# A conformer block on one core: full chunks' rows transposed by VectorE and DMAs in place of TensorE

## The chip, the core and the metric

The kernel runs on one NeuronCore of a Trainium2 chip. The time is device microseconds of one execution of the whole program. Three runs of the kernel before took 914.69, 914.84 and 915.0 us; the median is 914.84 us.

The engines are named as the profile names them: PE (TensorE, matrix multiplication; PEld is its loading of weights), ACT (ScalarE), DVE (VectorE), POOL (GpSimd), SP (SyncE, which here only issues DMAs). Results of PE go to PSUM, eight banks of 512 float32 per partition. Everything else lies in SBUF, 128 partitions.

## What is computed

A block of a speech encoder over x of 2 sequences x 4000 tokens x 144 features, 4 heads, all tensors in bf16:

```python
h = _layernorm(x); x = x + 0.5 * (_silu(h @ w_ff1a) @ w_ff1b)        # 144 -> 576 -> 144
h = _layernorm(x); qkv = h @ w_qkv                                   # 3 x 144, 4 heads of 36
p = _softmax(einsum('bhqd,bhkd->bhqk', q, k) * 36 ** -0.5)           # 4000 x 4000 per head
x = x + einsum('bhqk,bhkd->bhqd', p, v) @ w_o
h = _layernorm(x) @ w_pw1; h = h[..., :144] * _sigmoid(h[..., 144:])
x = x + _silu(depthwise_conv5(h, dw)) @ w_pw2                        # 5 taps along the tokens
h = _layernorm(x); x = x + 0.5 * (_silu(h @ w_ff2a) @ w_ff2b)
return _layernorm(x)
```

## The kernel before

**Tiling.** The 8000 tokens are 16 chunks of 500 (8 to a sequence); a chunk is four blocks of 125 tokens. X holds rows: 125 partitions, one token each, 144 features along. A layer norm (`ln`, line 704) takes sums with `bn_stats` on DVE, the inverse root as a power on POOL, and writes normalised rows XN. In the "calm" stages (the front, until keys and values of all eight chunks of the first sequence are there; and the tail, after the last score tile) DVE writes XN; between them POOL does, with 224 instructions in all.

**Transposing.** Every matmul that contracts over the features wants them on partitions. So `transp` (line 693) turns the rows: per block two PE transposes, 125 tokens x 72 features to 72 x 125, into one PSUM bank; then one copy of 72 x 1000 by DVE (ACT in calm stages where it is freer) to XT, or to XTQ for the projections. `ln_tr` and `ln_trq` (lines 749, 756) call it on normalised rows; `post1` (line 1089) calls it on AN, the attention's output rows. The features lie as 72 + 72, and each product is two matmuls of contraction 72 (`mm2`, line 783). The identity the transposes multiply with is IDENT; IDF is its float32 copy, made by one DVE cast in the setup and used in `epilogue` (line 1292), which turns the attention's sums back to rows, divides them and writes AN.

**Attention.** A score tile is 64 keys x 500 queries x 4 heads: four matmuls PS<-QT,KT into two banks, which run side by side on quarters of the array. `emit_exp` (line 1371) takes the exponential of both banks in one ACT instruction, 128 x 1000, into PT; four matmuls PS<-PT,VA then add weighted values in banks 6 and 7. Some tiles go to DVE instead (`dve_tile`, line 1385): five DVE instructions build the exponential as a sum of two parts from the bits of an int16, and since that gives two PT buffers, eight PS<-PT,VA matmuls follow in place of four. Of 992 full tiles ACT takes 825 and DVE 167.

**The order of the work** is made while the program is built. A planner (`Rec`, line 51; `Sched`, line 259) keeps a clock per engine, a cost per instruction, and how long after it a result can be read. Everything but the attention is written as generators ("threads") that ask for an engine and buffers; `pick_any` (line 1524) chooses at each step a score tile, an exp, a value product, or a thread's next piece. `due` (line 1611) says when a tile goes to DVE. What is chosen is appended to that engine's list. On the chip each engine works its own list in order, and an instruction waits for the semaphores of those it depends on. POLICY (line 373) holds the tables by which the planner chooses, one value for each 21 score tiles; FJ and TJ break ties in the front and the tail. Where the planner sees PE wait in the calm stages it fills in dummy matmuls PS<-IDENT (`warm`, line 611).

**Setup.** Lines 568 to 600: SP loads X of the first eight chunks, ACT's queue the first weights, POOL and DVE clear buffers, DVE makes IDF. POOL's list then goes on with the powers of the first layer norms.

**The SP queue** issues X's loads and the late weights until 22 us, then only the output's stores.

The transposing before, whose callers hand it rows and a place:

```python
for k in range(2):
    for i in range(n):
        op("pe", "transpose", ps[:, k, i, 0:rows], src[:, i, k * HD:(k + 1) * HD], IDENT[0:rows, 0:rows],
           r=[rk, "ID"], w=[("ps", bk)], cost=0.055, kind="f")
yield need("dve", hold=True)
copy(dst.rearrange("p k (i n) -> p k i n", i=n), ps[:, :, :, 0:rows], [("ps", bk)], wk, 2 * n * TB, 2.0, flex())
```

All engines' instructions are issued through one helper, so that the profile has them under one line (L170); groups are told apart by their tiles.

Of the kernel before, what the change touches and what calls it, by code (L numbers as in the profile page):

```python
# [12 lines left out]
D = 144  # L13
H = 4
DH = 36
# [27 lines left out]
def c_act(n):  # L43
    return n / 1200 + 0.051
# [6 lines left out]
class Rec:  # L51
# [6 lines left out]
    SWITCH = 0.095  # L58
# [12 lines left out]
    def op(self, eng, name, *a, r=(), w=(), q=None, cost=0.1, kind=None, lat=None, **k):  # L71
# [29 lines left out]
        if eng == "pe":  # L101
            if kind != self.kind:
                start += self.SWITCH
            self.kind = kind
# [4 lines left out]
        self.ops.append(o)  # L109
        return o  # L110
# [141 lines left out]
class Thread:  # L252
    def __init__(self, gen, ready, rank, no=0):
        self.no = no
        self.gen, self.ready, self.live, self.rank = gen, ready, True, rank
        self.req = None
# [67 lines left out]
def bass_standalone__conformer_family_zipformer__speech_kernel(  # L324
# [28 lines left out]
    def sb(name, shape, dt=BF16):  # L353
# [5 lines left out]
    NAN = 5  # L359
    TJ = (  # L360
        0.0, -0.6, 0, 0.0, -0.3, 0.0, 0.0, 0.0, 0.0, -0.6, 0.15, 0.15, -0.6, 0.0, 0.15, 0,
        0.0, 0.0, 0.0, 0.0, 0.0, 0.0, 0.3, 0.6, 0.6, -0.3, -0.3, 0.0, 0.0, 0.0, 0.0, 0.0,
        0.0, 0.0, 0.0, 0.15, 0.0, 0.0, 0.0, -0.15, 0.0, 0.0, 0.0, 0.0, 0, 0.6, 0.0, 0.0,
    )
    FJ = (
        0.0, 0.0, 0.0, 0.0, 0.0, 0.0, 0.0, 0.0, 0.0, 0.0, 0.0, 0.0, 0.0, 0.0, 0.0, 0.0,
        0.0, 0.0, 0.0, 0.0, 0.0, 0.0, 0.0, 0.0, 0.0, 0.0, 0.0, 0.0, 0, 0.0, 0.0, 0.0,
        -0.25, 0.0, 0.0, 0.0, 0.0, 0.0, 0.0, 0.0, 0.0, 0.0, 0, 0.0, 0.0, 0.0, 0.0, 0.0,
        0.0, 0.0, 0.0, 0.0, 0.0, 0.0, 0.0, 0.0, 0.0, 0.0, 0.0, 0.0, 0.0, 0.0, 0.0, 0.0,
    )  # L370
# [4 lines left out]
            0.56, 0.56, 0.56, 0.85, 0.85, 0.85, 0.56, 0.56, 0.56, 0.56, 0.56, 0.56, 1.0, 1.0, 0.56, 0.56,  # L375
            0.56, 0.56, 0.56, 0.56, 0.56, 0.56, 0.56, 0.56, 0.56, 0.6, 0.6, 0.5, 0.5, 0.5, 0.5, 0.56,
            0.56, 0.56, 0.56, 0.56, 0.56, 0.56, 0.56, 0.56, 0.5, 0.5, 0.56, 0.56, 0.56, 0.56, 0.56, 0.56,
            0.56,
        ),
        "DSLACK": (  # L380
            0.4, 0.4, 0.4, 2.5, 1.5, 1.5, 1.5, 1.0, 1.0, 1.5, 0.8, 0.4, 0.4, 0.4, 0.2, 0.2,
            0.4, 0.4, 0.4, 0.4, 1.5, 1.5, 1.5, 1.5, 4.0, 4.0, 4.0, 0.4, 0.4, 0.2, 0.4, 0.4,
            0.4, 0.4, 0.4, 0.4, 0.4, 0.4, 0.2, 0.2, 0.2, 0.4, 0.4, 0.4, 0.4, 1.5, 1.5, 1.5,
# [3 lines left out]
            2.0, 2.0, 4.0, 3.5, 4.5, 4.5, 4.5, 2.5, 2.5, 2.5, 2.5, 2.5, 2.5, 2.5, 2.5, 2.5,  # L387
            2.5, 2.5, 2.5, 2.5, 4.5, 2.5, 2.5, 2.5, 2.5, 2.5, 3.0, 3.25, 3.25, 3.0, 6.0, 3.25,
            3.25, 3.25, 3.25, 3.25, 4.0, 2.5, 2.5, 2.5, 3.25, 3.25, 3.25, 4.5, 4.5, 4.5, 3.25, 3.25,
# [3 lines left out]
            3, 3, 1, 1, 4, 4, 1, 1, 1, 3, 0, 0, 0, 0, 1, 1,  # L393
            1, 1, 1, 1, 1, 1, 1, 1, 1, 1, 1, 2, 1, 1, 1, 1,
            1, 1, 1, 1, 1, 1, 0, 0, 0, 0, 0, 1, 2, 0, 0, 1,
            1,
        ),
        "OBATCH": (
            1, 1, 2, 1, 1, 1, 1, 1, 1, 1, 1, 1, 1, 1, 1, 1,
            1, 1, 1, 1, 1, 1, 1, 1, 0, 2, 2, 2, 2, 2, 2, 1,  # L400
            1, 1, 1, 1, 1, 1, 2, 1, 1, 1, 1, 1, 1, 1, 3, 2,
            2,
        ),
        "LATE": (
            0.3, 0.3, 0.3, 0.3, 0.6, 0.6, 0.1, 0.2, 0.2, 0.2, 0.2, 0.2, 0.6, 0.6, 0.6, 0.1,
            0.1, 0.1, 0.1, 0.1, 0.1, 0.3, 0.3, 0.3, 0.3, 0.3, 0.2, 0.2, 0.2, 0.3, 0.3, 0.3,
            0.3, 0.3, 0.2, 0.2, 0.2, 0.2, 0.2, 0.2, 0.2, 0.2, 0.2, 0.2, 0.2, 0.2, 0.2, 0.2,
# [3 lines left out]
            1.8, 1.8, 1.6, 1.6, 1.6, 1.6, 1.6, 2.0, 2.5, 2.5, 2.5, 2.5, 2.5, 1.4, 2.5, 2.5,  # L411
            2.5, 1.8, 2.5, 2.5, 2.5, 1.6, 1.6, 1.6, 1.6, 1.6, 1.6, 1.4, 1.4, 1.4, 1.4, 3.5,
            3.5, 3.5, 3.5, 2.5, 2.5, 1.4, 1.4, 1.4, 1.6, 1.6, 3.0, 3.0, 1.4, 1.4, 1.4, 1.8,
# [3 lines left out]
            2, 2, 2, 2, 2, 2, 2, 2, 2, 3, 3, 3, 3, 3, 2, 2,  # L417
            5, 5, 4, 2, 2, 3, 2, 2, 2, 2, 2, 2, 2, 4, 2, 4,
            4, 5, 5, 2, 2, 2, 4, 5, 5, 5, 5, 5, 5, 5, 5, 4,
            3,  # L420
        ),
        "LIVE": (
            3, 3, 2, 2, 1, 1, 1, 1, 1, 2, 2, 2, 2, 3, 3, 3,
            3, 2, 2, 2, 2, 3, 3, 2, 2, 1, 1, 2, 2, 3, 3, 3,
            3, 3, 3, 3, 3, 3, 2, 3, 3, 4, 3, 3, 3, 3, 3, 3,
            3,
        ),
        "MAXQ": (
            2, 2, 3, 3, 1, 1, 3, 2, 1, 1, 1, 1, 1, 1, 3, 2,
            3, 3, 2, 2, 1, 2, 2, 2, 2, 1, 1, 2, 2, 2, 2, 2,  # L430
            2, 2, 2, 2, 2, 2, 3, 1, 1, 1, 3, 3, 3, 3, 3, 3,
            3,
        ),
        "EARLY": (
            2, 2, 2, 1, 3, 3, 2, 2, 2, 2, 2, 2, 2, 1, 1, 1,
            2, 2, 1, 1, 2, 2, 2, 2, 2, 2, 2, 2, 2, 2, 2, 2,
            2, 1, 1, 2, 2, 2, 3, 3, 3, 3, 3, 3, 2, 2, 2, 2,
# [3 lines left out]
            0.12, 0.12, 0.12, 0.12, 0.05, 0.05, 0.3, 0.12, 0.12, 0.05, 0.05, 0.05, 0.05, 0.05, 0.12, 0.12,  # L441
            0.12, 0.12, 0.12, 0.12, 0.12, 0.12, 0.12, 0.12, 0.12, 0.12, 0.12, 0.12, 0.2, 0.2, 0.2, 0.12,
            0.3, 0.2, 0.2, 0.2, 0.2, 0.2, 0.12, 0.12, 0.12, 0.12, 0.12, 0.12, 0.12, 0.12, 0.12, 0.12,
            0.12,
        ),
        "TWIN": (
            0.1, 0.1, 0.1, 0.1, 0.1, 0.1, 0.1, 0.1, 0.1, 0.1, 0.1, 0.1, 0.1, 0.1, 0.1, 0.1,
            0.1, 0.1, 0.1, 0.1, 0.1, 0.1, 0.1, 0.1, 0.0, 0.0, 0.0, 0.1, 0.1, 0.1, 0.1, 0.1,
            0.1, 0.1, 0.1, 0.1, 0.1, 0.1, 0.1, 0.1, 0.1, 0.1, 0.1, 0.1, 0.1, 0.1, 0.1, 0.1,
            0.1,  # L450
        ),
        "BGPICK": (
            0, 0, 0, 0, 0, 0, 0, 0, 0, 0, 0, 0, 0, 0, 0, 0,
            0, 0, 0, 0, 0, 0, 0, 0, 0, 0, 0, 0, 0, 0, 0, 0,
            1, 1, 1, 0, 0, 0, 1, 0, 0, 0, 0, 0, 0, 0, 0, 0,
# [3 lines left out]
            2, 2, 2, 1, 2, 2, 2, 2, 2, 0, 0, 0, 0, 0, 2, 2,  # L459
            2, 2, 2, 2, 2, 2, 2, 2, 2, 2, 2, 2, 2, 2, 0, 0,  # L460
            2, 2, 2, 2, 2, 3, 2, 2, 2, 2, 2, 2, 2, 2, 2, 2,
            2,
        ),
        "FDVE": (
            5, 5, 5, 5, 5, 5, 5, 5, 5, 5, 5, 5, 4, 4, 4, 5,
            5, 3, 3, 3, 3, 5, 5, 5, 5, 5, 5, 5, 5, 2, 2, 5,
            5, 5, 5, 5, 5, 5, 5, 5, 5, 5, 5, 5, 5, 1, 5, 5,
            5,
        ),
        "PRELAG": (  # L470
            0.7, 0.7, 0.7, 0.7, 0.7, 1.0, 0.7, 1.5, 1.5, 0.7, 0.7, 0.7, 0.7, 0.7, 0.7, 0.7,
            0.7, 0.7, 0.7, 0.7, 0.7, 0.7, 0.7, 0.7, 0.7, 0.7, 0.7, 1.0, 1.0, 1.0, 1.0, 0.7,
            0.7, 0.5, 0.5, 0.5, 0.5, 0.5, 0.7, 0.3, 0.3, 0.3, 0.7, 0.7, 0.5, 0.5, 0.5, 0.5,
            1.0,
        ),
        "LAGD": (
            1, 1, 1, 1, 1, 1, 1, 0, 0, 0, 0, 0, 1, 1, 0, 1,
            1, 1, 1, 1, 1, 1, 1, 1, 1, 1, 1, 1, 1, 0, 0, 0,
            1, 1, 1, 1, 1, 1, 1, 1, 1, 1, 1, 0, 0, 0, 0, 1,
# [19 lines left out]
    XN = sb("XN", [NXN, NB, D])  # L499
# [4 lines left out]
    XT = sb("XT", [NXT, 2, CW])  # L504
# [11 lines left out]
    AN = sb("AN", [NAN, NB, D])  # L516
# [24 lines left out]

    PS = nc.alloc_psum_tensor("PS", [128, 8 * 512], F32)
# [14 lines left out]

    def load_x(eng, c, r=()):
        load(eng, f"x{c}", X[0:TB, c * NB:(c + 1) * NB, :], x_tok[c], [("X", c, i) for i in range(NB)], r, 2.9)

    def load_ff(eng, qa, qb, WA, WE, WB, wa, wb, nm, la=None, lb=None):
        load(eng, qa, WA[0:HD, :, :], kh(wa)[:, :, 0:512], [(nm, "a", 0)], lat=la)
        load(eng, qa, WE[0:HD, :, 64:128], kh(wa)[:, :, 512:FF], [(nm, "a", 1)], lat=la)
        load(eng, qb, WB[:, 0:4, :], wb[0:512, :].rearrange("(t p) d -> p t d", p=128), [(nm, "b", 0)], lat=lb)
        load(eng, qb, WB[0:64, 4, :], wb[512:FF, :], [(nm, "b", 1)], lat=lb)
        load(eng, qb, WB[64:128, 5, :], wb[512:FF, :], [(nm, "b", 2)], lat=lb)

    load_x("sp", 0)
# [7 lines left out]
    op("pool", "memset", NHALF[:, :], -0.5, w=["NHALF"])  # L576
    op("pool", "memset", WP2Z[:, :, :], 0.0, w=[("WP2Z", i) for i in range(NB)], cost=0.3)
    op("pool", "memset", U2[:, :, :], 0.0, w=["U20"], cost=0.6)
    load("sp", "w2", WO[0:HD, :, :], kh(w_o), ["WO"])
    load("sp", "w2", WP1[0:HD, :, :], kh(w_pw1), ["WP1"])  # L580
# [9 lines left out]
    for WE, WB, nm, eng in ((WE1, WB1, "W1", "dve"), (WE2, WB2, "W2", "pool")):  # L590
        op(eng, "memset", WE[0:HD, :, 0:64], 0.0, w=[(nm, "a", 2)], cost=0.15)
        op(eng, "memset", WE[0:HD, :, 128:192], 0.0, w=[(nm, "a", 3)], cost=0.15)
# [61 lines left out]
    def setup_dw():  # L654
        for ab in range(2):
            op("dve", "tensor_copy", WPZ[0:HD, :, 48 + 64 * ab:64 + 64 * ab], WP1[0:HD, :, ab * D + ML:(ab + 1) * D],
               r=["WP1", "WPZ0"], w=["WPZ"], cost=0.15)
# [35 lines left out]
    def transp(src, rk, dst, wk, n, rows=TB):  # L693
        bk = yield need("pe", banks, dur=0.11 * n)
        ps = PSH[0:HD, bk, 0:256 * n].rearrange("p (k i n) -> p k i n", k=2, i=n)
        for k in range(2):
            for i in range(n):
                op("pe", "transpose", ps[:, k, i, 0:rows], src[:, i, k * HD:(k + 1) * HD], IDENT[0:rows, 0:rows],
# [1007 lines left out]
```

## Time and profile before

| | |
|---|---|
| median of 3 runs | 914.84 us (914.69 to 915.0) |
| the profiled execution | 914.9 us, its span 913.1 us |
| TensorE clock granted | 0.999 |
| ACT, exp of 128 x 1000 | 825 instructions, 768.8 us busy |
| PE, PS<-QT,KT and PS<-PT,VA | 3968 and 4636 instructions, 415.6 and 396.1 us busy |
| PE, transposes PS<-IDENT,XN and PS<-IDENT,AN | 512 and 128 instructions |
| DVE, copies XT<-PS and XTQ<-PS of 72 x 1000 | 51 and 8 instructions, mean 673 and 671 ns |
| DVE, the exps' three kinds of instruction | 222.4 + 134.7 + 113.0 us busy |
| DMA | 7322 packets, 7.36 MB |

How to read it: busy time of a group is the time in which at least one of its instructions is running, so instructions that overlap in a pipeline are not counted twice; the mean is that of a single record and holds its latency. The "idle before" column tells how long the engine had stood still ahead of the group and what ended that. A stretch's row gives, for every engine, the busy time in that stretch and the number of instructions. The chain of waits goes back from the last instruction, at each step to what released it.

### The profile page before, as it was taken

Reading aid. Unit: us, or ns where it says so; the run is one execution under the profiler, and the core shown is the slowest. Engines: PE = TensorE matmul, PEld = TensorE weight load, DVE = VectorE, ACT = ScalarE, POOL = GpSimd, SP = SyncE. Lnnn points to the kernel's source line nnn. Section 1 sums busy time; section 2 is a strip of 40 time slices with the busy share of each in tenths; the row PEclk is TensorE's granted clock in tenths of the full one; section 3 lists DMA queues with packets and bytes.
Section 4 is the critical chain, followed back from the end, with each engine's and each line's share of the span. In section 5 each row is a group of like instructions: output and inputs, shape, how many; then the busy total and the mean of one; then the engine's idle time right before and its main releaser. Section 6 shows DMA issues by size and latency. Waiting matters only on the chain.

```text
span 913.1 us, 27439 instructions
## 1 busy us (share of the span) xinstructions
PE 890.1 (97%) x11946; PEld 411.2 (45%) x11946; DVE 802.0 (88%) x1756; ACT 872.9 (96%) x1105; POOL 277.5 (30%) x519
## 2 busy tenths in 40 slices
PE   8999999999999999999999999999999999999996
PEld 7544434444444444444444444444434344444455
DVE  8988898898989999898988799897889699978987
ACT  5899999999999999999999999999999999999984
POOL 5121041145111612223415333240605050403143
PEclk9999999999999999999999999999999999999999
DMA  4000000000000000000000000000000000000000
GB/s 114 34 2 1 2 2 1 1 3 1 3 3 1 3 2 2 2 3 1 2 2 14 1 9 8 8 2 1 15 1 2 8 9 2 8 1 8 2 8 26
DMA packets 7322, 7.36 MB, mean 8 GB/s; under 512 B 2376, under 2 KB 7202, under 8 KB 7202
## 3 DMA queue, kind: packets, MB, share of 16 engines
q1 hardware_dynamic: 5786, 5.00, 1.8%
q8 instruction: 93, 1.52, 0.7%
q10 hardware_dynamic: 1416, 0.62, 0.3%
q14 instruction: 27, 0.22, 0.1%
HBM read 3.31 MB, written 2.30 MB: 6 GB/s over the span
## 4 chain that ended last, share of the span: by engine, by line
ACT 51%; PE 43%; DVE 4%; issue 1%; DMA 0%; POOL 0%; POOLq 0%; DVEq 0%
ACT PT L170 46%; PE PS L170 43%; ACT TH L170 5%; DVE HT L170 1%; DVE PT L170 1%; DVE ST L170 1%; DMA X<-in_x_dram 0%; DVE X L170 0%; DVE XN L170 0%; DVE QT L170 0%; POOL RS L170 0%; DVE XT L170 0%; DVE RS L170 0%; DVE SW L170 0%; DVE VA L170 0%
## 5 line engine op out<-in xcount | busy, mean ns | idle before, releaser
L170 ACT ACTIVATE PT<-PS 128x1000 bf16<-128x1000 f32 (+1 forms) x841 | 777.2, 1050 | 8.3 <-PE PS L170 5.9
L170 PE MATMUL PS<-QT,KT 64*64 64x500 bf16 x3968 | 415.6, 383 | 8.6 <-ACT PT L170 5.6
L170 PE MATMUL PS<-PT,VA 64*37 64x500 bf16 x4636 | 396.1, 373 | 1.9 <-DVE QT L170 1.4
L170 DVE TENSOR_SCALAR PT<-PS 128x500 int16<-128x500 f32 x334 | 222.4, 671 | 31.5 <-PE PS L170 29.5
L170 PEld LDWEIGHTS PS<-QT,KT 64*64 64x64 bf16 x3968 | 123.8, 104 | 195.7 <-ACT PT L170 112.5
L170 PEld LDWEIGHTS PS<-PT,VA 64*37 64x37 bf16 x4636 | 132.1, 95 | 111.3 <-issue 26.7
L170 POOL TENSOR_SCALAR RS<-ST 125x4 f32<-125x4 f32 x112 | 36.6, 327 | 471.0 <-DVE ST L170 465.8
L170 DVE TENSOR_SCALAR PT<-PT 128x1000 uint16<-128x1000 uint16 x334 | 134.7, 416 | 1.3
L170 POOL TENSOR_SCALAR XN<-X,RS 125x144 bf16<-125x144 bf16 x224 | 131.8, 599 | 5.8
L170 POOL TENSOR_TENSOR RS<-RS,NHALF 125x4 f32<-125x4 f32 (+2 forms) x101 | 94.1, 936 | 101.6 <-DVE RS L170 96.9
L170 DVE TENSOR_TENSOR PT<-PT 128x1000 bf16<-128x1000 bf16 x167 | 113.0, 681 | 1.5
L170 ACT ACTIVATE TH<-PS 128x500 bf16<-128x500 f32 (+3 forms) x198 | 104.3, 552 | 6.7 <-PE PS L170 5.6
L170 DVE SCALAR_TENSOR_TENSOR HT<-TH,PS 128x500 bf16<-128x500 bf16 (+1 forms) x135 | 80.6, 616 | 25.1 <-ACT TH L170 24.4
L170 PE MATMUL PS<-XT,WA 72*128 72x500 bf16 (+2 forms) x280 | 74.3, 360 | 0.6 <-DVE VA L170 0.3
L170 DVE SCALAR_TENSOR_TENSOR X<-PS,X 125x288 bf16<-125x288 f32 x128 | 57.4, 452 | 14.8 <-PE PS L170 13.1
L170 DVE BATCH_NORM_STATS2 ST<-X 125x6 f32<-125x288 bf16 (+1 forms) x160 | 65.8, 447 | 1.0 <-DMA X<-in_x_dram 0.8
L170 PE MATMUL PS<-WB,HT 128*125 128x144 bf16 (+1 forms) x640 | 52.7, 230 | 0.3 <-DVE HT L170 0.3
L170 PEld LDWEIGHTS PS<-WB,HT 128*125 128x125 bf16 (+1 forms) x640 | 44.3, 136 | 14.8 <-issue 3.8
L170 PE MATMUL PS<-IDENT,XN 125*72 125x125 bf16 x512 | 42.4, 221 | 1.5 <-DVE XN L170 0.9
L170 DVE COPY XT<-PS 72x1000 bf16<-72x1000 bf16 (+2 forms) x65 | 39.9, 617 | 3.3 <-PE PS L170 2.5
L170 PEld LDWEIGHTS PS<-IDENT,XN 125*72 125x72 bf16 x512 | 31.5, 112 | 20.2 <-issue 12.6
L170 PE MATMUL PS<-U,DG 128*128 128x250 bf16 (+5 forms) x204 | 34.3, 265 | 0.1
(86 smaller groups left out, 560.6 us busy)
## 6 DMA issues: line engine op xcount, KB each, us to landing
X<-in_x_dram SPq DMA_DIRECT2D x16, 140.6 KB
out_dram<-XN SPq DMA_DIRECT2D x14, 140.6 KB
WA<-in_w_ff1a_dram ACTq DMA_DIRECT2D x1, 144.0 KB
WB<-in_w_ff1b_dram ACTq DMA_DIRECT2D x1, 144.0 KB, 2.6
WA<-in_w_ff2a_dram SPq DMA_DIRECT2D x1, 144.0 KB
WB<-in_w_ff2b_dram SPq DMA_DIRECT2D x1, 144.0 KB
out_dram<-XN SPq DMA_DIRECT2D x2, 70.3 KB
WQKV<-in_w_qkv_dram ACTq DMA_DIRECT2D x1, 121.5 KB
```

The source lines that it names most:

```text
L170: ins = getattr(eng, o.name)(*o.a, **o.k)
```

## The change

Full chunks outside the calm stages no longer go through PE to be transposed. POOL (XN) and `epilogue` (AN) write their rows so that two blocks' tokens alternate: element (feature f, block j of a pair) at 2f + j. Two bf16 neighbours are one four-byte word, a chunk is 125 x 288 words, padded with cleared columns and rows to 128 x 320. One DVE instruction, `transpose` on the float32 view, turns every 32 x 32 block of words in place. Four DMAs write the result to a scratch in DRAM (each takes 32 partitions and writes runs of 32 words, 128 bytes), and, when these have landed, two DMAs read it back with the features on partitions: 128 + 16 of them to XT, 72 + 72 to XTQ. All six are issued by SP. In XT the columns of such a chunk alternate between two blocks, and matmuls read them with a step of two (`xt`), or in pairs' order for the output (`by_block`); in XTQ the order of tokens within a chunk is kept as it comes, and `epilogue` undoes it (`otf`).

All products from XT now split the features 128 + 16, the second part's contraction being 80 rows of which 64 are zero (cleared weights and XT). So weights are loaded in two DMAs each, and more buffers are cleared in the setup: on DVE the second halves of WA1 and WE1, WE1's borders, XN (1600 words) and the second half of XT (1280 words); on POOL those of WO, WP1, WA2 and WE2, and AN (2560 elements). In the calm stages PE still transposes, to 128 and 80 rows, and two copies follow in place of one.

The planner's costs for switches on PE are finer (`bub`), AN has four buffers in place of five, a rule keeps short background bursts back (BURST, BAGE), and all tables of POLICY, FJ and TJ are new, so the whole order of all engines' lists is. Instruction counts of the two programs:

| engine, instruction | before | after |
|---|---|---|
| PE transposes of rows | 640 | 168 |
| PE PS<-PT,VA | 4636 | 4684 |
| ACT exp 128 x 1000 | 825 | 813 |
| ACT TH<-PS 128 x 500 | 138 | 136 |
| DVE score tiles | 167 | 179 |
| DVE copies XT, XTQ of 72 x 1000 | 59 | 0 |
| DVE transpose of 128 x 320 words | 0 | 59 |
| SP writes to and reads from the scratch | 0 | 236 and 118 |
| PE dummy matmuls | 156 | 185 |

```diff
-    NAN = 5
+    NAN = 4
...
-    XN = sb("XN", [NXN, NB, D])
+    XNS = sb("XN", [NXN, 640])
+    XN = XNS[:, :, 0:NB * D].rearrange("p u (i d) -> p u i d", i=NB)
+    XNI = XNS[:, :, :].rearrange("p u (g f j) -> p u g f j", g=2, j=2)
...
-    XT = sb("XT", [NXT, 2, CW])
+    XT = sb("XT", [NXT, 2, NB, 128])
+    XTJ = XT[:, :, :, :, :].rearrange("p s k i n -> p s k (i n)").rearrange("p s k (g n j) -> p s k g n j", g=2, j=2)
...
+    DR = nc.dram_tensor("rows", [NXT + CPB, 5, 32, 2, 4, 32], F32).ap().rearrange("z k r g a n -> z k r a g n")
...
+    def load_k(eng, q, W, wap, w, zero, lat=None):
+        load(eng, q, W[:, 0, :], wap[0:128, :], [w], lat=lat)
+        load(eng, q, W[0:LC, 1, :], wap[128:D, :], [("rest", w)], r=[zero], lat=lat)
...
+    KK = (128, LP)
...
+    zero_k("dve", WA1, ("W1", "z", 0))
+    zero_e("dve", WE1, "W1")
+    op("dve", "memset", XNS[:, :, :], 0.0, w=[("XN", u) for u in range(NXN)], cost=0.9)
+    op("dve", "memset", XT[0:LP, :, 1, :, :], 0.0, w=[("XT", u, i) for u in range(NXT) for i in range(NB)], cost=0.75)
...
+    zero_k("pool", WO, "WOZ")
+    zero_k("pool", WP1, "WP1Z", 0.25)
+    zero_k("pool", WA2, ("W2", "z", 0), 0.4)
+    zero_e("pool", WE2, "W2")
...
+    op("pool", "memset", ANS[:, :, :], 0.0, w=[("AN", a) for a in range(NAN)], cost=1.6)
...
+    SP_COST = 0.36
+    W_LAT = 2.0
+    T_LAT = 2.4
+
+    def blocks(v, key, z, reads, q, wk):
+        yield need("dve")
+        op("dve", "transpose", v, v, r=[key], w=[key], cost=c_dve(320))
+        yield need("sp")
+        first, v = None, v.rearrange("p (g k n) -> p g k n", g=2, n=32)
+        for a in range(4):
+            args = "sp", "dma_start", DR[z, :, :, a, :, :].rearrange("k r g n -> r g k n"), v[32 * a:32 * a + 32, :, :, :]
+            if first is None:
+                first = op(*args, q=f"d{z}", r=[key], w=[("DR", z)], cost=SP_COST, lat=W_LAT)
+            else:
+                R.more(first, [key], [("DR", z)], *args, q=f"d{z}", cost=SP_COST, lat=W_LAT)
+        first, d = None, DR[z, :, :, :, :, :].rearrange("k r a g n -> (k r) g a n")
+        yield need("sp")
+        for dst, f0, f1, n in reads:
+            args = "sp", "dma_start", dst, d[f0:f1, :, :, :].rearrange("f g a n -> f g (a n)")[:, :, 0:n]
+            if first is None:
+                first = op(*args, q=q, r=[("DR", z)], w=wk, cost=SP_COST, lat=T_LAT)
+            else:
+                R.more(first, [("DR", z)], wk, *args, q=q, cost=SP_COST, lat=T_LAT)
...
+    def transp(u, an, s, bs, inter, dma, rows=TB):
+        n, key = len(bs), ("AN" if an else "XN", u)
+        wk = [("XT", s, i) for i in bs]
+        x_inter[s] = dma
+        if dma:
+            yield from blocks((ANF if an else XNF)[:, u, :], key, s,
+                              [(XTF[0:128, s, 0, :, :], 0, 128, 128), (XTF[0:16, s, 1, :, :], 128, D, 128)], f"t{s}", wk)
+            return
...
     def ln_tr(c, s, bs, e=False):
-        u = yield from ln(c, bs, e)
...
+        inter = len(bs) == NB and not calm()
+        u = yield from ln(c, bs, e, inter)
+        yield from transp(u, False, s, bs, inter, inter and not calm(), TB + e)
         xnp.give(u)
...
-            op("pe", "matmul", PSV[0:rows, bk, 0:CH], lhsT=W0[0:HD, k, m0:m1], rhs=XT[0:HD, s, k, 0:CH], start=k == 0,
-               stop=k == 1, r=[("XT", s, i) for i in range(NB)] + wk, w=[("ps", bk)], cost=c_pe(CH), kind="f")
+            op("pe", "matmul", by_block(PSV[0:rows, bk, 0:CH], 2), lhsT=W0[0:KK[k], k, m0:m1], rhs=xt(s, k, 0, NB), start=k == 0, stop=k == 1, r=[("XT", s, i) for i in range(NB)] + wk, w=[("ps", bk)], cost=c_pe(CH), kind="f")
...
+        if ok and R.kind == "q" and (s or o) and sum(q[2].req.dur for q in ok) < now("BURST") and min(
+                q[2].since for q in ok) > R.free["pe"] - now("BAGE"):
+            ok = []
```

(The copying of `transp` and its twin `transp_q`, `xt`, `by_block`, `otf` and the tables are left out here.)

## The prediction

> **What bounds the kernel now.** I read the page's engine line and slices first, then busy time by stretch, then the chain of waits.
>
> ```profile
> PE 890.1 (97%) x11946; PEld 411.2 (45%) x11946; DVE 802.0 (88%) x1756; ACT 872.9 (96%) x1105; POOL 277.5 (30%) x519
> ...
> ACT  5899999999999999999999999999999999999984
> ```
>
> ```profile
> core 0: us, PE busy (x) PEld busy (x) DVE busy (x) ACT busy (x) POOL busy (x), PEclk, DMA share, GB/s
> 20.00:50.00 30.00, 28.68 (x304) 15.18 (x296) 28.20 (x78) 24.14 (x43) 6.83 (x11) 1.00 0.11 38
> 50.00:125.00 75.00, 74.08 (x1049) 31.36 (x1050) 63.18 (x158) 73.63 (x89) 9.88 (x15) 1.00 0.01 2
> 125.00:875.00 750.00, 738.99 (x10012) 325.17 (x10011) 667.54 (x1372) 742.76 (x913) 236.48 (x444) 1.00 0.02 4
> 875.00:913.10 38.10, 30.69 (x371) 23.79 (x363) 27.48 (x93) 21.51 (x42) 13.61 (x25) 0.97 0.07 20
> ```
>
> ```profile
> 679.89 26.00 ACT PT L170 x29
> ...
> 771.31 23.09 ACT PT L170 x26
> ```
>
> Three stages are to be seen. In the front (to about 50 us) nobody is full except DVE. From 50 to 875 us ACT is busy 816.4 of 825 us: 8.6 us idle in all. PE is busy 813.1 of the same 825, so two engines are full at once, and DVE follows at 89%. After 875 us comes a tail of 38 us in which ACT is busy 21.5. In the chain, long pieces are exps of ACT one behind the other: 23.09 us for 26 is 0.888 us for one (a record of 1050 ns overlaps the next). So in the middle only two things shorten the run: fewer ACT instructions, or ACT's last few idle microseconds.
>
> **The change, part by part.** Counts come from the two kernels' instruction lists; durations are starts' distances in the trace, or groups' means.
>
> 1. *PE.* 640 transposes become 168: 472 fewer. Eight of them hold PE 0.63 us in the timeline, of which about 0.17 is the last one's latency: 0.057 each, 27 us off PE. Twelve more score tiles take the VectorE exp, which costs four more PT,VA matmuls each (16 such hold PE about 0.85 us, so 0.053 each): +48, 2.5 us. Net -24 us. No engine waits for this by itself; it lets the list feed ACT better.
>
> 2. *ACT, first exp to last.* Exps 825 to 813: -12 x 0.888 = -10.7. TH of 500 columns -4 x 0.47 = -1.9. The other small differences (copies of XT, KT, XTQ, VA, one TH of 80 rows) add up to +0.9. Sum -11.7 us, on the path, as ACT is full there.
>
> 3. *ACT's idle time.* From the first exp to the last it is about 14.5 us (6 of them before 50 us). With 24 us off PE part of it should go. Bounds: 8 us less, or 10 us more if PE's new waits reach ACT. I take -3, nearer the gain, because PE is what ACT's few waits there are for (5.9 us before PT), and PE loses work.
>
> 4. *DVE.* Out: 51 + 8 copies of 72x1000 (671 ns mean, 0.59 apart), -35 us. In: 12 VectorE exps (two of 0.59, two of 0.33, one of 0.60: 2.4 us each), +29; 59 transposes of 128x320 words of four bytes, which no row shows. Bounds: 0.26 us apart if two words go per cycle as in the copies, 0.74 if one takes two cycles. The nearest row, 500 float32 from PSUM in 671 ns, is one word per cycle: 0.40, so +24. Sum +18 us (+9 to +38). DVE then runs at about 93% in the middle: hidden behind ACT, but with less cover. At 0.74 it is 95%, and ACT would wait for it.
>
> 5. *DMA, new.* Each transposed chunk needs four writes, a wait, two reads, all issued by SP, which does nothing else from 22 to 482 us. Least: four issues of 0.26 (stores' median) + landing 1.7 (X<-X) + two issues of 0.26 + landing 1.7 = 5.0 us. Most: four of 0.41 (X loads) + 3.1 (the final wait for the stores) + two of 0.41 + 2.8 (WB) = 8.4.
>
> ```profile
> q1 hardware_dynamic: 5786, 5.00, 1.8%
> ...
> X<-X SPq DMA_DIRECT2D x1, 0.6 KB, 1.7
> ```
>
> ```profile
> SPq L176 <- DMA out_dram<-XN: 3.1, 3, 1.5
> ```
>
> Packets add to it: 1.8% of 16 engines over 913 us for 5786 packets is 45 ns each; the writes are 1280 runs of 128 bytes, 80 an engine, 3.6 us against 1.0 to 1.7 us of issuing. So up to 1.9 more: 5.0 to 10.3. I take 6.7. Its cover: the lists fix what stands between a transpose and the first matmul that reads its result. Weighted with the pitches of the trace (0.21 us for 500 columns), PE's list holds, from the last matmul that the transpose surely follows, less than 7 us in 5 of the 59 cases, less than 8 in 19, less than 9 in 26, less than 10 in 31. So 6.7 us is hidden nearly everywhere. Beyond it the shortfalls add up to 15 us at 8, 37 at 9, 65 at 10. Queued behind a waiting SP are only other chunks' writes and the stores; behind a waiting PE stand the next scores, and so ACT.
>
> 6. *Front.* DVE gets five memsets ahead of the first statistics (3.3 thousand words in all; one of 176 takes 0.20 us, so about 3.4 us) and POOL six (3.8 thousand elements; 576 take 0.58 us, so 3.8; two that go had taken 0.35).
>
> ```profile
> 1.53 2.53 DVE L170 CAST IDF<-IDENT 128x128 f32<-128x128 bf16 x1
> ...
> 3.45 0.52 POOL L170 MEMSET WK<- 128x512 bf16 x1
> ...
> 4.84 0.82 DVE L170 BATCH_NORM_STATS2 ST<-X 125x6 f32<-125x288 bf16 x2 [0.79 <-DMA X<-in_x_dram]
> ```
>
> (Timeline: start, duration, engine.) POOL's memsets now end at 3.97 and its power for the first chunk starts at 5.82; with 3.5 us more they end at 7.4, so that power, and all behind it, is at least 1.6 us later. And the cast, 128 words a partition that the later memsets of 128 words do in 0.17 us, lasted until POOL's last memset ended: if that is no accident it ends at 7.5 and the statistics start 2.7 us late. I take +2.6 (1.6 to 3). [...]
>
> 7. *Calm stages* (front to about 125 us, and tail) keep PE's transposes, but each now needs two copies (128 and 80 rows) for one: about 0.1 us more at some 20 places of the front, half of it hidden: +1 (0 to 2.5).
>
> 8. *Tail.* One more chunk's convolution and projection falls behind the last exp: 23 more matmuls (2.1 us of PE), a handful of ACT instructions, and the list shows 26 more filler matmuls, 1.5 us that PE is to stand by. ACT and PE have room there (30.7 and 21.5 of 38). +1.5 (-2 to +4).
>
> Sum: -11.7 - 3 + 2.6 + 1 + 1.5 = -9.6 us. The profiled execution took 914.9 us (span 913.1 and 1.8 around it); the median of the runs is 914.84, the same within 0.1. So **905.3 us**. Its own range, from the ends of 3, 6, 7 and 8, is 898 to 911.
>
> **Rivals.**
>
> *More gain* (0.11). Two full engines hindered each other; with PE off the edge ACT's idle goes by 8 us or more, the front's memsets overlap: 893 to 898. For it: PE loses twice what ACT does. Against: 8.6 us idle of 825 is little to win.
>
> *No gain* (0.14). VectorE takes PE's place: the transposes take 0.74 us, or POOL's row work (131.8 us) and DVE hold each other up; the 12 us off ACT come back as waits for DVE. 911 to 916. For it: 93% on DVE. Against: where ACT waits now, it is for PE.
>
> *Slower: the rows come back late* (0.16). The chunk's way through DRAM takes 8 us or more. Every late XT stops PE's list at a fixed place, ACT runs dry after the one or two tiles that lie ready, and nothing overtakes. It decides from about 7.6 us on, where the shortfalls reach 10 us. At 8 us 905.3 + 15 = 920, at 9 us 942, at 10 us 970. For it: writes of 128 bytes, two landings in line, half of the cases with under 10 us of cover. Against: 6.7 us from rows. [...]
>
> *Slower: strided reading* (0.04). The chunks that go through DRAM lie in XT with every second column belonging to another block, so 312 matmuls of 500 and 250 columns and 120 of 125 read with a step of two: 150 thousand columns, 63 us at 0.21 for 500. At half rate PE has 739 - 24 + 63 = 778 us in the middle, 40 more than the 738 left to it by the forecast: some 945. No row of before shows such a step over many columns.
>
> The change doing less than it says is excluded: the lists show the transposes gone.
>
> **Chances.** Forecast 0.55, more gain 0.11, no gain 0.14, late rows 0.16, strided reading 0.04. A measurement of this kernel tells about 0.2% (1.8 us) from no change. Faster by more: 0.55 + 0.11 + just over half of no gain, 0.74; within: 0.06; slower: 0.20. Range: 896 to 924 us leaves out half of more gain, most of late rows above 8.2 us, and strided reading: about 0.19.
>
> **What would show it.** ACT busy from 125 us on at 99% with about 813 exps: steps 2 and 3. DVE's transpose rows at about 0.48 us: step 4. The rows' way, from DVE's transpose to the landing of the second read, at or under 7 us, and PE waiting for DMA under 5 us in all: step 5; tens of microseconds there mean late rows. First statistics near 7.5 us instead of 4.84, with a cast that ends with POOL's last memset: step 6. From ACT's last exp to the end 35 us now, 36 to 37 then: step 8. Matmuls PS<-XT,WA of 500 columns still 0.21 us apart: no strided cost. Wrong altogether would be a span in which ACT stands idle by more than 25 us between its first and last exp.

## The result, and the profile after

The changed kernel took 925.77 us (median of four runs, 924.34 to 928.14) beside 914.82 us for the kernel before: a ratio of 1.0122, 95% interval 1.0097 to 1.0147. It is 11 us slower; 905.3 was forecast. The profiled execution took 924.55 us, with a span of 922.7 us. Its page: engines first, then the shares of the chain that ended last. The last line is that chain's in the kernel before.

```profile
PE 883.4 (96%) x11559; PEld 394.0 (43%) x11559; DVE 814.8 (88%) x1836; ACT 868.5 (94%) x1109; POOL 279.8 (30%) x519
...
PE 42%; ACT 31%; DVE 17%; DMA 4%; SPq 2%; POOL 2%; issue 1%; POOLq 0%; DVEq 0%
```

```profile
ACT 51%; PE 43%; DVE 4%; issue 1%; DMA 0%; POOL 0%; POOLq 0%; DVEq 0%
```

ACT's share of the chain has fallen from 51 to 31%, DVE's has grown from 4 to 17%, and DMA and SP's queue are in it now. The busy time by stretch, in the columns that the prediction showed:

```profile
core 0: us, PE busy (x) PEld busy (x) DVE busy (x) ACT busy (x) POOL busy (x), PEclk, DMA share, GB/s
20.00:50.00 30.00, 27.49 (x318) 16.81 (x316) 28.59 (x88) 22.32 (x45) 7.84 (x12) 1.00 0.11 39
50.00:125.00 75.00, 72.76 (x1049) 32.15 (x1046) 66.06 (x170) 72.02 (x90) 13.80 (x22) 1.00 0.01 2
125.00:875.00 750.00, 725.48 (x9512) 299.91 (x9508) 665.83 (x1400) 734.11 (x896) 227.20 (x423) 1.00 0.13 28
```

From 125 to 875 us ACT is idle 15.9 us (7.2 before) and PE 24.5 (11.0 before). The next two rows, of before and of after, cut at the start of the first and at the end of the last exp of 1000 columns:

```profile
20.59:877.39 856.80, 843.55 (x11371) 372.43 (x11367) 759.36 (x1605) 842.68 (x1044) 254.81 (x472) 1.00 0.02 5
```

```profile
23.44:885.21 861.77, 831.59 (x10928) 350.88 (x10928) 766.78 (x1669) 835.13 (x1033) 254.17 (x469) 1.00 0.12 26
```

By these the 9.6 us of span lie as follows (all in us):

| profiled execution | to first exp | first to last exp | ACT busy there | ACT idle there | after last exp |
|---|---|---|---|---|---|
| before | 20.59 | 856.8 | 842.7 | 14.1 | 35.7 |
| after | 23.44 | 861.8 | 835.1 | 26.6 | 37.5 |

The front and the tail came out as forecast (+2.85, +1.8). In the middle ACT has 7.5 us less to do, and stands idle 12.5 us longer. What it waits for between 23 and 880 us (columns: us in total, times, longest), before and after:

```profile
ACT PT L170 <- PE PS L170: 5.6, 18, 0.6
ACT TH L170 <- PE PS L170: 4.2, 6, 1.1
```

```profile
ACT PT L181 <- PE PS L181: 11.1, 30, 1.3
ACT TH L181 <- PE PS L181: 6.4, 11, 1.7
```

ACT waits for PE, although PE has 387 matmuls fewer. And PE, in the same window, waits for something that the kernel before did not have:

```profile
PEld PS L181 <- DMA XT<-rows: 10.6, 11, 2.3
PE PS L181 <- DMA XT<-rows: 6.4, 7, 1.9
PEld PS L181 <- DMA XTQ<-rows: 2.3, 3, 1.8
PE PS L181 <- DMA XTQ<-rows: 1.4, 1, 1.4
```

A row of PEld and one of PE may tell of the same wait: a matrix multiplication and the loading of its weights stand still together, and in the timeline each of the 8 waits of PE lies inside one of the 14 of PEld. So the four rows don't add up. There are 14 places; the loading of weights stands 13.0 us there, and PE itself 7.8 us (6.4 + 1.4), up to 1.9 us at a time. Why rows come late shows on SP. The first fence is a transpose on DVE, the second SP's queue around it (start, duration, engine, what, count):

```profile
274.94 0.51 DVE L181 STREAM_TRANSPOSE AN<-AN 128x320 f32<-128x320 f32 x1
```

```profile
273.67 0.61 SPq L181 DMA_DIRECT2D rows<-XN  x1
276.44 1.69 SPq L181 DMA_DIRECT2D XTQ<-rows  x2
278.17 2.60 SPq L181 DMA_DIRECT2D rows<-AN  x4
282.18 0.81 SPq L181 DMA_DIRECT2D XT<-rows  x2
```

The transposed rows are ready at 275.45, but SP stands still until 276.4, waiting for the writes of the chunk ahead to land, then issues that chunk's reads; the new chunk's writes start at 278.17, 2.7 us late. Four writes take 2.6 us to issue: 0.65 apart. The way from the transpose's end to the second read's landing (its issue + 2.0, the page's median landing) has a median of 7.3 us over the 59 chunks, and is over 8 us in 19 of them. In the median chunk SP begins the writes at once (0.03 us after the transpose); the longest delay is 4.3 us.

The planner inside the kernel has figures of its own for this: SP_COST 0.36 for an issue, W_LAT 2.0 and T_LAT 2.4 for the landings. Measured against the list made with them, 22 of the 59 chunks land more than 0.5 us later than the list counts on.

### The profile page after: what moved, and what is told of

It is laid out like the page before. It is cut to its first block, busy times and chain, and to the rows that moved or that the text cites. A ratio compares the mean times of both kernels' runs of the same rounds, so it can differ in the third digit from the quotient of the medians.

```text
span 922.7 us, 27119 instructions
## 1 busy us (share of the span) xinstructions
PE 883.4 (96%) x11559; PEld 394.0 (43%) x11559; DVE 814.8 (88%) x1836; ACT 868.5 (94%) x1109; POOL 279.8 (30%) x519
## 4 chain that ended last, share of the span: by engine, by line
PE 42%; ACT 31%; DVE 17%; DMA 4%; SPq 2%; POOL 2%; issue 1%; POOLq 0%; DVEq 0%
PE PS L181 42%; ACT PT L181 28%; DVE PT L181 7%; ACT TH L181 3%; DVE ST L181 2%; SPq L181 2%; DMA XT<-rows 2%; DVE XN L181 2%; DVE QT L181 2%; DMA rows<-XN 1%; DVE HT L181 1%; DVE X L181 1%; POOL RS L181 1%; POOL XN L181 1%; DMA rows<-AN 1%
## 5 line engine op out<-in xcount | busy, mean ns | idle before, releaser
L181 ACT ACTIVATE PT<-PS 128x1000 bf16<-128x1000 f32 (+1 forms) x829 | 768.6, 1025 | 14.9 <-PE PS L181 11.2
L181 PE MATMUL PS<-PT,VA 64*37 64x500 bf16 x4684 | 421.0, 374 | 2.1 <-DVE QT L181 0.6
L181 DVE TENSOR_SCALAR PT<-PS 128x500 int16<-128x500 f32 x358 | 237.0, 669 | 22.0 <-PE PS L181 20.9
L181 PEld LDWEIGHTS PS<-PT,VA 64*37 64x37 bf16 x4684 | 137.4, 95 | 129.8 <-DVE PT L181 32.8
L181 DVE TENSOR_SCALAR PT<-PT 128x1000 uint16<-128x1000 uint16 x358 | 143.1, 416 | 1.0
L181 DVE TENSOR_TENSOR PT<-PT 128x1000 bf16<-128x1000 bf16 x179 | 120.9, 680 | 1.1
L181 DVE SCALAR_TENSOR_TENSOR HT<-TH,PS 128x500 bf16<-128x500 bf16 (+1 forms) x135 | 81.1, 617 | 23.8 <-ACT TH L181 23.5
L181 PE MATMUL PS<-XT,WA 128*128 128x500 bf16 (+4 forms) x288 | 76.1, 364 | 3.7 <-DMA XT<-rows 2.5
L181 POOL COPY U<-U 128x2 bf16<-128x2 bf16 (+1 forms) x54 | 13.1, 276 | 77.0 <-DVE U L181 77.0
L181 PEld LDWEIGHTS PS<-XT,WA 128*128 128x128 bf16 (+1 forms) x288 | 20.3, 98 | 37.7 <-issue 12.6
L181 DVE TENSOR_SCALAR XN<-X,ST,RS 125x144 bf16<-125x144 bf16 (+1 forms) x96 | 25.0, 312 | 1.9 <-POOL RS L181 1.7
```

Source lines behind the costliest of these rows:

```text
L181: ins = getattr(eng, o.name)(*o.a, **o.k)
```

## The experiments

**Theory A**, the list: the new order is itself what leaves ACT idle. **Rival B**, late rows: PE's waits for DMA pass on to ACT. **Rival C**, VectorE in PE's place. Every kernel keeps the list of its parent unless said; all medians are beside the kernel before in the same session (914.6 to 915.0). The table cuts profiled executions as above (us):

| run | median | ratio, 95% interval | to first exp | first to last exp | ACT idle there |
|---|---|---|---|---|---|
| e1 free rows | 922.0 | 1.0077 (1.0065 to 1.0089) | 23.45 | 858.7 | 23.8 |
| e2 short transposes | 920.6 | 1.0060 (1.0048 to 1.0072) | 23.45 | 857.8 | 23.7 |
| e6 both | 917.0 | 1.0025 (1.0015 to 1.0035) | 23.45 | 852.8 | 19.7 |
| e4 list a | 920.1 | 1.0064 (1.0045 to 1.0084) | 23.43 | 856.0 | 23.2 |
| e12 list a, free rows | 913.3 | 0.9986 (0.9977 to 0.9995) | 23.43 | 848.4 | 16.7 |
| e10 list b | 911.6 | 0.9965 (0.9953 to 0.9978) | 23.43 | 849.0 | 16.4 |
| e11 list b, memsets spread | 909.9 | 0.9947 (0.9934 to 0.9961) | 21.93 | 848.6 | 16.0 |

**e1: rows not waited for.**

```diff
-            return XTJ[0:KK[k], s, k, i0 // 2:i1 // 2, 0:rows, :].rearrange("p g n j -> p g j n")
+            return WFJ[0:KK[k], k, i0 // 2:i1 // 2, 0:rows, :].rearrange("p g n j -> p g j n")
...
+    WFJ = WA1[:, :, :].rearrange("p k (g n j) -> p k g n j", g=2, j=2)
...
+            o.deps = [(d, raw) for d, raw in o.deps if d.q not in ("t0", "t1", "t2", "t3", "t4")]
```

> The changed kernel with the same list of instructions on every engine, but the 51 chunks that go through DRAM into XT are not waited for by TensorE: their matmuls read a finished weight tile of the same shape and step instead (so the output is made from other data). Transposes, writes and reads all stay, as do the eight XTQ chunks. Theory A (the list): the new order of instructions is itself what leaves ScalarE idle, and at this order the rows' way is hidden; then 923 to 926 us, at most 3 us less than the changed kernel's 925.8. Rival B (late rows): the 17 us in which TensorE waits for DMA pass on to ScalarE; then 909 to 916 us. Rival C (VectorE in TensorE's place): no change, 924 to 926.

922.0 us, 3.8 less: under A's range, above B's. Late rows cost something at this list. The 17 us of the expectation had added the waits of PEld and PE; PE itself had stood 6.4 us for the rows in XT, and ACT's idle time fell by 2.8 us. The difference of 3.8 us is known to some 2.5 us, as the changed kernel's four runs spread over 3.8.

**e2: VectorE's transposes all but gone.**

```diff
-        op("dve", "transpose", v, v, r=[key], w=[key], cost=c_dve(320))
+        op("dve", "transpose", v[0:32, 0:32], v[0:32, 0:32], r=[key], w=[key], cost=c_dve(320))
```

> The changed kernel with the same list, but each of the 59 VectorE transposes turns only one block of 32x32 words instead of 128x320 (39 of 40 blocks are left as they are), so VectorE has about 59 x 0.4 = 24 us less to do, and the writes start 0.4 us sooner. Theory A (the list): 923 to 926 us. Rival B (late rows): 0.4 us of 7 sooner, 2 to 5 us less, 921 to 924. Rival C (VectorE): at 90% busy it holds the scores' and exps' order up, and a good part of 24 us comes back: 908 to 917.

920.6 us, 5.2 less. More than A or B allow, less than C asks: a fifth of the 24 us comes back, though DVE was busy only 89% of the stretch from 125 to 875 us. Not all of it need be VectorE's: the rows leave sooner too, and PE waits 5.7 us for them in place of 7.8.

**e3: memsets late.**

```diff
+    late = [op("pool", "memset", ANS[:, :, :], 0.0, w=[("AN", a) for a in range(NAN)], cost=1.6),
+            op("pool", "memset", U2[:, :, :], 0.0, w=["U20"], cost=0.6)]
...
+    at = next(i for i, o in enumerate(R.ops) if o.eng == "pool" and o.t0 > 86)
+    R.ops[at:at] = late
```

> The changed kernel with the same list, but GpSimd's memsets of AN (2.23 us) and U2 (0.63 us) are taken out of the first 7 us and put after its power of about 97 us, where it stands idle for 15 us. By the step of the prediction on the front, GpSimd's last memset then ends about 2.9 us sooner, the cast and the first statistics are no longer blocked, and the first exp comes 2.0 to 2.7 us sooner: 923.0 to 924.0 us. Rival: what bounds the front lies behind the first chunk (later chunks' statistics and powers), and less than 0.7 us comes back: over 925. If VectorE is held up by the memsets where they now lie, up to 2 us of it is lost again.

926.4 us (924.9 to 927.5): no gain. The front did what it should, first exp at 21.90, 1.54 us sooner; but from there to the last exp the profiled run took 865.0 us, 3.2 more. Three rows of its timeline, one each from POOL, DVE and PE, show one place where it was lost:

```profile
83.37 2.23 POOL L181 MEMSET AN<- 128x2560 bf16 x1
```

```profile
83.78 2.66 DVE L181 TENSOR_SCALAR PT<-PT 128x1000 uint16<-128x1000 uint16 x1
```

```profile
87.53 1.44 PE L181 MATMUL PS<-PT,VA 64*37 64x500 bf16 x12 [1.98 <-DVE PT L181]
```

A DVE instruction that takes 0.42 elsewhere lasted 2.66 us beside the memset, and PE waited 1.98 us for it. From 88 to 91 us the granted clock was 0.51 (last section).

**e4: other tables** (list a). Only POLICY and TJ differ. The tables were found stage by stage, keeping the values whose list the planner's own clock puts ahead.

> The changed kernel with nothing altered but the planner's tables (POLICY and TJ), derived anew once more; so the same mechanism in another order. The planner's own clock puts this list 6.6 us below that of the changed kernel (900.5 against 907.1; for the kernel before it is 896.9). Theory A (the list): the measured time follows, 918 to 921 us. Rivals B and C (the rows' way, or VectorE, bound it whatever the order): 924 us or more, as there are as many transposes and a few more VectorE exps.

920.1 us, as A said. Order alone is worth 5.7 us here (its six runs spread from 918.2 to 924.9). But PE still stands 6.4 us for rows.

**e5 and e9: PE's relief alone, in the kernel before.** In e5 the transposes turn 8 tokens; in e9 seven of eight go. The edits of the copy, e5's and e9's, and e9's of the transposes (the lines of the copies are cut at their end):

```diff
-        copy(dst.rearrange("p k (i n) -> p k i n", i=n), ps[:, :, :, 0:rows],
+        copy(dst.rearrange("p k (i n) -> p k i n", i=n), ps[:, :, :, 0:1].to_broadcast([HD, 2, n, rows]),
...
+        copy(dst.rearrange("p k (i n) -> p k i n", i=n), ps[:, 0:1, 0:1, 0:rows].to_broadcast([HD, 2, n, rows]),
...
-                op("pe", "transpose", ps[:, k, i, 0:rows], src[:, i, k * HD:(k + 1) * HD], IDENT[0:rows, 0:rows],
+                o = op("pe", "transpose", ps[:, k, i, 0:rows], src[:, i, k * HD:(k + 1) * HD], IDENT[0:rows, 0:rows],
...
+                if n == NB and (k, i) != (0, 0):
+                    gone.append(o)
```

> The kernel before, same list, but the 59 full chunks' transposes turn 8 tokens instead of 125 (117 of 125 tokens are left out, the copy out of PSUM reads one column again and again, at its old size). This takes the change's gain for TensorE alone: some 20 us off TensorE in the middle, nothing added. The prediction let ScalarE's idle time fall with it by 3 us (bounds: 8 less). Theory A (nothing waits for TensorE as a sum; the order decides): 912.5 to 915 us. Rival (TensorE bounds beside ScalarE): 905 to 910.

931.9 us, 17 *slower*, outside both ranges. The cause is an accident of the edit. The copy's row in e5, then in e9 (673 ns in the kernel before):

```profile
L170 DVE COPY XT<-PS 72x1000 bf16<-72x1000 bf16 x51 | 60.4, 1185 | 1.4 <-PE PS L170 1.3
```

```profile
L170 DVE COPY XT<-PS 72x1000 bf16<-72x1000 bf16 x51 | 34.6, 679 | 156.9 <-PE PS L170 156.9
```

Reading one column again and again nearly halved the copy's rate: 59 x 0.51 = 30 us more on DVE. So e5 measures VectorE in a kernel without any DMA way: 30 us more on DVE cost 17 us and the gain below.

> The kernel before, same list, but of the eight TensorE transposes of a full chunk seven are left out (59 chunks, 413 transposes of 0.057 us, 23 us off TensorE), and the copy out of PSUM reads the one transposed block eight times, with contiguous inner runs, so that it should keep its 0.67 us. Told apart by it: what TensorE's relief is worth alone, which the run with 8-token transposes did not tell, since its copies took 1.19 us each, 30 us more for VectorE. Theory A (no engine waits for TensorE as a sum): 912.5 to 915 us. Rival (TensorE bounds beside ScalarE): 905 to 910. If the copies are again slow, it shows in their row and the run tells nothing of this.

911.2 us (910.96 to 911.65; the profiled execution took 4306.8 us and is left out, and only the busy columns of its copy row are used). 23 us off PE give 3.6 us: between the two ranges. That is about all that the change's first step could bring at an unchanged order.

**e6: e1 and e2 together.**

> The changed kernel, same list, with both edits at once: TensorE waits for none of the rows that come back through DRAM (the eight XTQ chunks now too), it reads a finished weight tile in their place, and VectorE turns one block of 32x32 instead of the chunk. All DMAs stay. If late rows and VectorE's transposes are separate costs, they add: 3.8 + 5.2 and a little for XTQ, 915 to 917 us. If both only feed the same few late places, 919 to 921. If these two were the whole loss against the forecast, the middle would be the forecast's: 905 to 910 us; what lies between 910 and the measured time is then the list's.

917.0 us, 8.8 less: 3.8 + 5.2 add up within the scatter of the runs, so they are in the main separate costs. How much of the second is VectorE's own stays open. e6 frees the XTQ rows as well, for which PE still stood 2.6 us in e1, with 3.4 us at half clock behind it; from e1 to e6 it is 5.0 us for both together. 917.0 is still 12 above the forecast, and these two do not explain that.

**e7: a longer way.**

```diff
-        for a in range(4):
-            args = "sp", "dma_start", DR[z, :, :, a, :, :].rearrange("k r g n -> r g k n"), v[32 * a:32 * a + 32, :, :, :]
+        for a in range(8):
+            d = DR[z, :, :, a // 2, :, :].rearrange("k r g n -> r g k n")
+            args = "sp", "dma_start", d[a % 2 * 16:a % 2 * 16 + 16], v[16 * a:16 * a + 16, :, :, :]
```

> The changed kernel, same list, but each chunk is written to DRAM by eight DMAs of 16 partitions instead of four of 32, same bytes and packets; the trace shows SyncE's issues of these writes 0.65 us apart, so the rows' way, 6.4 us now from the transpose's end to the second read's landing, becomes 1.5 to 2.6 us longer, 8 to 9 us. The prediction put the shortfall at 15 us of time at a way of 8 us and 37 at 9. Theory B (the way is only just covered): 940 to 965 us, and the granted clock falls in more windows, as it did in the runs with TensorE waits of 1.6 to 2.1 us. Theory A (hidden with room to spare): below 930.

1012.1 us (1006.8 to 1022.5): B's sign, and well over its range. Half the bytes did not make an issue cheaper: from 120 to 200 us eight writes take 5.1 to 6.0 us, 0.64 to 0.76 each, beside 0.65 before. The way's median is 10.4 us, 52 of 59 chunks over 9. PE's waits and the granted clock in 40 slices:

```profile
PEld PS L181 <- DMA XT<-rows: 62.0, 25, 6.9
PE PS L181 <- DMA XT<-rows: 48.3, 21, 6.5
```

```profile
PEclk9999979898988998999999989999999999999999
```

With the XTQ rows (18.5 us of PEld, 16.1 of PE) the loading of weights stands 80.5 us and PE itself 64.5, in the same places. Up to the last exp the clock is at half for 71.7 us (and 3.4 at the very end, where every run has 3 to 6.5), which costs at most half of that, 36 us of PE's work, as an estimate from the granted clock.

**e8: the kernel before with the changed kernel's POLICY.**

> The kernel before, its own transposes and nothing of the new way, but with the changed kernel's POLICY tables (without the two keys that it does not have). The planner's own clock ends 39 us later for this list, 936.0 against 896.9. Theory A (the order of the list is worth tens of microseconds by itself): 950 to 957 us. Rival (tables are fine adjustment): under 925.

952.5 us (two runs), as A said: 38 us from tables alone, with none of the new way in the kernel.

**e10: the tables and the way's figures** (list b; the new POLICY and TJ, and the lines that use the four figures, are not shown).

```diff
-    SP_COST = 0.36
-    W_LAT = 2.0
-    T_LAT = 2.4
+    W_COST = 0.65
+    T_COST = 0.38
+    W_LAT = 1.4
+    T_LAT = 2.6
```

> The changed kernel with nothing altered but the planner's tables and its four figures for the rows' way, which follow the trace now (a write's issue 0.65 us instead of 0.36, then 1.4 to its landing; a read's issue 0.38, then 2.6), so that its list keeps what reads the rows later. The planner's own clock ends at 899.3. If the late rows and the order are what the changed kernel lost by, TensorE waits for DMA under 10 us in all (19 now), no window at half clock in the middle, and 915 to 918 us. Rival (VectorE bounds, whatever the order): 920 or more.

911.6 us: 14.2 less than the changed kernel, faster than the kernel before, better than expected. In the middle the clock never falls. What PE still waits for rows, and the middle by stretch:

```profile
PEld PS L181 <- DMA XT<-rows: 2.7, 4, 1.1
PE PS L181 <- DMA XT<-rows: 1.1, 2, 0.8
PEld PS L181 <- DMA XTQ<-rows: 0.3, 1, 0.3
```

```profile
125.00:875.00 750.00, 732.71 (x9663) 306.92 (x9656) 677.53 (x1426) 741.52 (x909) 226.96 (x442) 1.00 0.13 29
```

ACT's idle time here is 8.5 us of 750, near the 7.2 of the kernel before, and PE itself stands 1.1 us for rows in place of 7.8. The rows' way is no shorter: median 7.1 us, 20 chunks over 8 us. But only 6 land more than 0.5 us later than this list counts on (22 in the changed kernel, 24 in list a).

**e12: list a, rows not waited for.** As e1, on list a, the XTQ rows included.

> The kernel of e4_list_a, same list, but TensorE waits for none of the rows that come back through DRAM; its matmuls read a finished weight tile of the same shape (so the output is made from other data), the eight XTQ chunks included. All transposes and DMAs stay. It tells why the list of e10_list_b (911.6 us), whose planner's end is only 1.2 us lower, is 8.5 us faster than that of e4_list_a (920.1): if it is the rows that come later than the list's own figures count on, 911 to 914 us here; if it is the rest of the order, 917 to 920.

913.3 us: the first of the two, late rows. Without them list a is 6.8 us faster, most of the 8.5 us between lists a and b.

**e11: list b, the memsets spread.**

```diff
+    late = [op("pool", "memset", ANS[:, a, :], 0.0, w=[("AN", a)], cost=0.4) for a in range(NAN)]
+    late.append(op("pool", "memset", U2[:, :, :], 0.0, w=["U20"], cost=0.6))
...
+    for o, t in zip(late, (33, 47, 55, 60.2, 90)):
+        at = next(i for i, p in enumerate(R.ops) if p.eng == "pool" and p.t0 > t)
+        R.ops.insert(at, o)
```

> As e10_list_b, and GpSimd's memsets of AN's four buffers and of U2, some 0.6 us each, spread one by one over its idle places between 30 and 90 us instead of in one row ahead of the first power. The earlier run with these memsets late had the first exp 1.5 us sooner and lost it again where one memset of 2.23 us stopped VectorE and, behind it, TensorE for 2.0 us, with 3.4 us at half clock after it. If that was the whole loss, 1.2 to 1.6 us less than e10_list_b; if the short memsets stop VectorE as well, no gain.

909.9 us, 1.7 less than list b; the first exp at 21.93. This version beats both kernels: 4.9 us faster than before.

## Why the prediction was wrong, point by point

- *Step 1, PE.* The counts were right, the size was not: between first and last exp PE's busy time fell by 12.0 us (843.55 to 831.59), not by 24, and no run tells what took the other half. That PE's relief is not itself on the path was nearly right: e9 gives 3.6 us for 23.
- *Step 2, ACT.* 12 exps fewer, as counted; ACT's busy records between first and last exp fell by 7.5 us, not 11.7.
- *Step 3, ACT's idle time: the step that failed.* −3 was taken, +10 was the bound, +12.5 came: 15.5 us of the 20 by which the forecast missed. The 26.6 us of idle time are also more than the 25 that the prediction had named as the sign of being wrong altogether. The reason given, that ACT waits for PE and PE loses work, counted PE's work, and neither PE's new waits nor the new list. The planner's own clock had it the other way: it ends at 896.9 us for the list before and at 907.1 for the new one (expectation of e4), 10.2 later, and the chip's span grew by 9.6. Between first and last exp the planner, run from the two kernels, has 845.0 us before and 851.1 after, and ACT idle 28.0 and 43.6 us. (It counts no overlap of ACT's instructions, so only the differences compare with the trace: +6.1 for the stretch, measured +5.0; +15.5 of idle time, measured +12.5.) So most of the idle time stands in the list itself. The two planners price PE's switches differently, so this is a strong sign and not a proof; that order moves the time is shown by e4 and e8.
- *Step 4, VectorE.* The duration was right (0.50 us a record; 0.48 forecast), the sum was not: DVE's busy time between first and last exp rose by 7.4 us, not 18, and from 125 to 875 us it was busy 89%, not 93%. "Hidden behind ACT" was wrong too: e2 gives back 5.2 of 24 us, e5 takes 17 for 30. Even at 89% an engine that hands tiles to PE and ACT in a fixed order is no free cover.
- *Step 5, the rows' way.* "I take 6.7 … hidden nearly everywhere" failed as well, at a smaller price. The sum for one chunk alone was fair (6.4 us where SP is free). It took an issue at 0.26 to 0.41 us, where a write's is 0.65, and it priced chunks one by one, where SP serves them in line and stands still at each wait. So 19 of 59 chunks took over 8 us, nearly all inside the stated bound of 10.3 (the longest 10.7). The rival "rows come back late", given 0.16, named this and a time of 920 at a way of 8 us. The measured 925.8 lies near that, but partly by luck: taking the waits for XT's rows away (e1) gives back 3.8 of the 20 us. Its price was too low where it was tested: 970 was said for 10 us, e7 took 1012 at 10.4.
- *Step 6, the front,* +2.85 (forecast 2.6, or 2.7 with the cast blocked). The cast ended with POOL's last memset, as it did before:

```profile
4.85 2.33 DVE L181 CAST IDF<-IDENT 128x128 f32<-128x128 bf16 x1
```

```profile
6.59 0.52 POOL L181 MEMSET WK<- 128x512 bf16 x1
```

- *Step 7* cannot be told apart in these runs. *Step 8:* +1.8, forecast +1.5.
- *Strided reading* did not happen: two matmuls of 500 columns take 0.63 us together, 0.60 before. The second starts 0.237 us after the first where columns are read with the step, 0.222 before: some 7% dearer, not double.

The prediction read the cover of each chunk off the list, but not against what the list had been made to expect. The kernel holds those figures in plain sight (0.36 us for an issue). The trace of before has no such write; its nearest issues, 0.26 to 0.41 us, were what the sum used, and they seemed to bear the kernel's figure out. With the figures set right and the tables derived anew (e10) the change gains 3.2 us, and with its front mended (e11) 4.9 of the 9.6 forecast. Shown are: late rows, 3.8 us at the changed kernel's list and 6.8 at list a; VectorE's transposes with the 0.4 us by which their rows then leave sooner, 5.2; order, 5.7 (list a) in the changed kernel and 38 in the kernel before; the memsets, 1.7. Why the best list still is 4.6 us above the forecast, and how far VectorE's share stands behind that, stays open; no run held the one and varied the other.

## What to carry to other kernels

Where a kernel follows a list made ahead, a new latency does harm by being longer than the list counts on, not by its length: list b has the same 7 us as the changed kernel and a seventh of PE's waits (1.1 us, 7.8 there). Before such a change, read the planner's own end for both lists; compare its figures with rows of the trace, above all for the issuing queue; and count the chunks that queue there at once. And removing work from an engine at 98% gives little (3.6 us for 23 in e9, where nothing was added elsewhere) when the engine next to it is full as well.

## What the runs showed of the hardware

**A short wait of PE can cost twice.** In the run of list a, PE waits 2.1 us for rows; the stretches before, during, and after, with the granted clock in the third column from the right:

```profile
177.00:180.80 3.80, 3.78 (x68) 1.32 (x58) 3.72 (x8) 3.80 (x6) 0.00 (x0) 1.00 0.34 71
180.80:184.00 3.20, 1.08 (x14) 0.25 (x10) 1.73 (x4) 1.54 (x3) 0.00 (x0) 1.00 0.17 51
184.40:187.60 3.20, 3.20 (x34) 1.60 (x32) 1.83 (x4) 2.31 (x4) 0.00 (x0) 0.50 0.01 3
188.00:191.00 3.00, 3.00 (x52) 1.38 (x48) 2.87 (x7) 3.00 (x4) 0.00 (x0) 1.00 0.02 5
```

After the wait PE issues 34 matmuls in 3.2 us instead of some 55. The half-clock stretch lasts 3.4 us, as do those in e1 and e3. Waits of 1.6 us (e1) and 1.98 us (e3) were followed by one too, and so were two waits of 0.38 and 0.81 us within two microseconds (e3, at 705 us) and one of 0.95 us (e5, at 500 us). Others as long were not: 1.86 and 1.38 us in the changed kernel, 1.70 in e2, 1.36 in list a. What decides between them no run here shows. PE was idle for 28 to 62% of the 3.4 us ahead of each of the five drops. The times of kernels with late rows also scatter more: the changed kernel's runs spread over 3.8 us, those of e6 and e12, which wait for no rows, over 0.9; that the clock is the reason is not shown.

**POOL's memset stops some DVE instructions and not others.** Beside the 2.23 us memset a DVE instruction of 0.42 us took 2.66 (e3). The cast of IDF, which in the changed kernel took 2.33 us and ended with POOL's last memset, took 0.23 in e3, where it starts at the same 4.85 us and POOL's memsets are over at 4.36. Memsets of DVE ran beside POOL's in the first 4 us: that of XT took 1.12 us beside POOL's 2.23 us memset of AN in the changed kernel, and 1.12 us in e3, where that one came later.

**A write to the scratch took SP no less to issue with 16 partitions than with 32**: 0.64 to 0.76 us (20 KB, e7, 120 to 200 us) beside a median of 0.64 (40 KB, the changed kernel), both in runs of 128 bytes; a read into XT took 0.4.
